# Two transformer layers, twice: all five queues, engine homes and PSUM banks of a written-out order replaced by another table

## The chip, the cores and the metric

One core of a Trainium2 chip runs the whole program. The metric is the device time of one execution in microseconds (us); 442.46 us is the median of three runs of the kernel before (442.39 to 442.56). The profile is one execution taken by the hardware profiler.

## The reference

The input is 2048 tokens of width 512 in bf16. A is sliding-window attention with 32 heads of width 16, B a gelu MLP of width 1792. Both come after a layer norm and are added to the residual:

```python
def _A_ref(x, wqkv, wo):                  # H = 32; Dh = 16; W = 256
    qkv = (x @ wqkv).reshape(B, S, 3, H, Dh).transpose(2, 0, 3, 1, 4)
    q, k, v = qkv[0], qkv[1], qkv[2]
    scores = einsum("bhqd,bhkd->bhqk", q, k) * (Dh ** -0.5)
    mask = (i - j >= 0) & (i - j < W)
    p = softmax(where(mask, scores, -1e9))
    return einsum("bhqk,bhkd->bhqd", p, v).transpose(...).reshape(B, S, D) @ wo
def _B_ref(x, w1, b1, w2, b2):            # 512 -> 1792 -> 512
    return gelu(x @ w1 + b1) @ w2 + b2
x = x + _A_ref(_layernorm(x), wqkv, wo)
x = x + _B_ref(_layernorm(x), w1, b1, w2, b2)
x = x + _A_ref(_layernorm(x), wqkv, wo)   # the same weights again
x = x + _B_ref(_layernorm(x), w1, b1, w2, b2)
```

## The kernel before

Everything stays in SBUF: the residual X (16 tiles of 128 tokens), all weights, and the intermediate buffers. The two repetitions are one stream of 32 tiles, handled as 16 attention blocks (0 to 15) of two tiles; blocks 0 and 8 are the first of a repetition.

For each block the steps are these. Two tiles are normalised on VectorE (statistics L599 and L601, xn L627; the reciprocal root in two small steps, L611 and L617, the second always on GpSimd) and transposed by DMA into xnTA (a few by TensorE). TensorE projects Q, K and V (L653, 256 columns for Q and K, 512 for V). VectorE takes K out of PSUM under a parity mask (KT, L687); Q and V leave PSUM by a copy on VectorE (L588) or on ScalarE (L590). Shifted copies of V go by DMA (Vs). The scores of a block are computed in ten visits (five in blocks 0 and 8), numbered from 0, each a group of small matmuls (L754) into four of the eight PSUM banks. Two exponentials on ScalarE (L761), one for each pair of banks, move a visit to the ring buffer E and free its banks. The window's edges are zeroed by masks (L782) on VectorE or on GpSimd. Two groups of probability matmuls for each block (L804, some 120 matmuls with their sums in a 17th column) write two banks; VectorE transposes them out (OD, L813), takes reciprocals (L817), VectorE or GpSimd normalises (Nb, L821), VectorE transposes back (OT, L827), TensorE projects with Wo (L653, out of OT) and VectorE adds the residual (X, L849).

The MLP runs in ten jobs of two or four tiles: normalisation and transposes into xnTB as above, W1 (L653, ps<-xnTB,W_sb) in 14 groups, gelu into gT (six groups over VectorE's bias add L871 and ScalarE's L874, eight by ScalarE with the bias, L879), W2 (L653, ps<-W_sb,gT, 14 steps for each tile), and the sum X = Xb + ps on VectorE (L894), where Xb, the residual with the bias b2, was prepared on GpSimd (L887). ScalarE changes its function table between exponentials and gelu, 19 loads in all. The last tile is computed in two halves of 256 columns. In the second repetition each finished tile is written out from the SP queue, which issues all DMAs.

What sets the order: the kernel first lists 3098 steps without an order, each with its engine, buffers, the PSUM banks it needs and those it frees. Three tables then decide everything. `_ORDER` is a permutation of the steps; each engine runs its own steps in that sequence. `_ALT` lists the steps that run on their second engine (their home): evacuations VectorE or ScalarE, masks, normalisation and the small L611 VectorE or GpSimd. `_BANKS` gives the first PSUM bank of each group, in the order of `_ORDER`. A step waits, by semaphores, for the last writers of what it reads and the last users of what it overwrites, banks included:

```python
for i in _ALT:
    nodes[i]["eng"], nodes[i]["fn"] = nodes[i]["alts"][1]
...
for i in _ORDER:
    nd = nodes[i]
    for g, k in nd["alloc"]:
        b = next(banks)
        gmap[g] = tuple(range(b, b + k))
    for g in nd["free"]:
        free.update(gmap[g])
```

TensorE has 1629 of the steps; a dense step is one to four matmuls of L653.

Of the kernel before, what the change touches and what calls it, by code (L numbers as in the profile page):

```python
# [19 lines left out]
class _Sched:  # L20
# [147 lines left out]
    15, 34, 5, 0, 6, 14, 35, 7, 33, 28, 38, 29, 47, 8, 18, 23, 9, 36, 3, 26, 31, 10, 57, 37, 11, 22, 1, 40, 4, 24,  # L168
    2, 58, 59, 61, 17, 42, 62, 21, 60, 65, 41, 63, 19, 64, 68, 55, 32, 66, 107, 39, 69, 67, 20, 105, 50, 70, 3097,
    48, 30, 27, 53, 25, 106, 108, 71, 109, 49, 72, 110, 73, 16, 74, 114, 81, 75, 82, 111, 83, 84, 115, 85, 86, 116,  # L170
    112, 87, 88, 89, 113, 195, 153, 117, 127, 128, 151, 196, 129, 130, 154, 118, 152, 131, 119, 197, 155, 120, 156,
    98, 99, 100, 121, 12, 101, 90, 13, 102, 367, 91, 368, 104, 159, 92, 93, 157, 94, 103, 325, 76, 369, 199, 77,
    326, 95, 78, 200, 79, 370, 132, 80, 133, 96, 134, 135, 201, 323, 97, 203, 198, 137, 136, 158, 138, 205, 144,
    139, 202, 140, 145, 204, 141, 146, 160, 147, 122, 520, 217, 148, 123, 206, 124, 219, 143, 125, 208, 126, 46,
    218, 324, 43, 213, 209, 327, 328, 215, 166, 167, 168, 331, 169, 214, 207, 371, 176, 329, 177, 521, 373, 210,
    178, 330, 216, 179, 522, 171, 172, 180, 372, 161, 173, 211, 142, 174, 170, 56, 375, 220, 162, 376, 332, 163,
    164, 523, 175, 524, 221, 374, 377, 150, 212, 165, 149, 380, 378, 222, 188, 382, 189, 44, 190, 181, 45, 525,
    182, 381, 223, 385, 183, 224, 191, 386, 184, 384, 226, 225, 227, 54, 231, 232, 387, 379, 233, 526, 234, 383,
    333, 228, 185, 343, 388, 389, 334, 192, 229, 235, 344, 395, 194, 230, 335, 396, 345, 238, 346, 291, 390, 236,
    397, 239, 237, 347, 240, 336, 241, 348, 337, 349, 338, 242, 350, 244, 339, 243, 391, 399, 351, 401, 340, 341,  # L180
    352, 400, 245, 403, 342, 392, 402, 51, 353, 405, 52, 354, 355, 398, 356, 186, 360, 404, 357, 361, 362, 527,
    363, 393, 408, 364, 253, 409, 260, 261, 407, 254, 262, 410, 359, 413, 255, 246, 247, 415, 411, 256, 412, 257,
    248, 249, 250, 258, 414, 406, 564, 251, 273, 394, 274, 566, 263, 276, 416, 267, 268, 417, 565, 264, 270, 271,
    265, 277, 642, 285, 286, 423, 567, 418, 640, 275, 643, 528, 287, 529, 428, 272, 419, 282, 252, 283, 429, 288,
    259, 289, 641, 420, 308, 290, 309, 421, 424, 266, 310, 311, 279, 278, 644, 269, 422, 645, 284, 307, 280, 312,
    281, 313, 314, 315, 540, 425, 426, 568, 427, 541, 570, 316, 648, 542, 543, 649, 317, 569, 544, 318, 530, 531,
    319, 532, 187, 533, 572, 534, 193, 320, 574, 321, 646, 430, 431, 322, 647, 292, 573, 293, 294, 432, 577, 295,
    435, 579, 366, 576, 296, 545, 297, 436, 358, 571, 298, 433, 578, 546, 582, 434, 547, 437, 584, 548, 575, 550,
    438, 899, 551, 552, 650, 583, 553, 439, 651, 441, 652, 440, 653, 554, 900, 897, 585, 592, 654, 299, 549, 300,
    301, 593, 365, 302, 303, 304, 442, 581, 305, 594, 586, 535, 536, 898, 580, 596, 537, 306, 598, 538, 587, 901,  # L190
    539, 902, 597, 595, 600, 588, 557, 601, 660, 661, 662, 663, 599, 602, 605, 664, 558, 559, 607, 560, 655, 656,
    561, 457, 458, 606, 603, 610, 903, 657, 589, 658, 612, 904, 604, 453, 590, 459, 454, 476, 455, 477, 611, 485,
    486, 563, 609, 479, 591, 480, 482, 562, 613, 659, 470, 471, 483, 556, 905, 464, 465, 467, 478, 468, 484, 608,
    450, 460, 469, 461, 906, 451, 466, 446, 452, 447, 481, 443, 487, 448, 444, 473, 472, 462, 665, 474, 456, 614,
    666, 667, 445, 463, 615, 449, 475, 616, 684, 625, 626, 668, 617, 489, 686, 620, 618, 490, 491, 492, 685, 493,
    619, 621, 494, 669, 688, 687, 627, 690, 628, 622, 629, 495, 488, 623, 689, 496, 632, 692, 497, 694, 498, 624,
    691, 499, 500, 501, 630, 502, 693, 697, 504, 631, 505, 633, 1017, 506, 698, 507, 508, 634, 509, 1018, 510, 503,
    635, 699, 511, 702, 1019, 670, 512, 704, 700, 671, 672, 1020, 695, 673, 1021, 703, 674, 712, 696, 513, 514,
    701, 676, 714, 515, 706, 516, 517, 705, 518, 713, 519, 716, 638, 707, 717, 715, 718, 833, 720, 708, 721, 677,
    917, 1022, 918, 919, 709, 722, 920, 719, 710, 725, 921, 678, 727, 679, 680, 724, 681, 726, 730, 922, 636, 923,  # L200
    1023, 731, 912, 924, 728, 1024, 913, 723, 914, 915, 732, 729, 925, 711, 941, 637, 943, 734, 907, 908, 909, 733,
    910, 916, 926, 555, 735, 942, 639, 1025, 911, 736, 945, 934, 946, 935, 675, 737, 947, 738, 683, 949, 1026, 936,
    739, 948, 951, 937, 740, 938, 741, 742, 682, 950, 743, 944, 954, 744, 745, 955, 746, 747, 750, 952, 748, 940,
    927, 749, 956, 959, 953, 928, 752, 929, 961, 930, 1037, 751, 1038, 753, 931, 1039, 754, 1040, 960, 755, 957,
    969, 970, 756, 758, 757, 963, 971, 973, 962, 1027, 1028, 1041, 974, 1029, 759, 1030, 1031, 958, 977, 978, 964,
    975, 787, 965, 788, 979, 789, 976, 790, 776, 782, 791, 982, 981, 777, 1274, 983, 778, 779, 972, 780, 984, 987,
    980, 783, 784, 988, 785, 966, 986, 765, 786, 766, 767, 985, 768, 989, 771, 769, 772, 773, 774, 991, 1061, 775,
    1063, 990, 1065, 967, 1067, 992, 968, 1062, 1276, 760, 761, 762, 1066, 993, 763, 803, 804, 805, 806, 1068,
    1277, 764, 1069, 798, 1070, 994, 799, 800, 1275, 995, 801, 818, 1071, 819, 820, 821, 1278, 808, 996, 849, 809,
    810, 811, 793, 997, 1279, 998, 999, 770, 794, 1064, 1000, 823, 1001, 795, 807, 796, 1002, 1072, 824, 797, 825,  # L210
    826, 1003, 781, 1004, 1005, 828, 1006, 829, 792, 1032, 1033, 1007, 830, 834, 1034, 822, 1282, 831, 835, 1009,
    1035, 812, 836, 1280, 837, 802, 813, 1010, 814, 1281, 1396, 815, 827, 816, 838, 1073, 839, 1008, 817, 1394,
    840, 1283, 841, 842, 832, 1011, 843, 1012, 844, 845, 1074, 933, 846, 847, 850, 848, 851, 1075, 932, 852, 853,
    1015, 854, 881, 855, 1036, 1076, 856, 1079, 1395, 1397, 857, 1080, 858, 1078, 1077, 859, 860, 882, 861, 1081,
    1089, 862, 863, 1090, 883, 1083, 1082, 884, 885, 864, 886, 1091, 887, 1093, 1042, 1043, 1095, 1092, 1044, 865,
    1045, 1084, 1046, 1094, 1097, 1085, 888, 1098, 889, 890, 891, 866, 1096, 1099, 867, 1086, 1102, 1398, 868,
    1399, 1103, 869, 892, 893, 1100, 894, 870, 1104, 895, 1107, 896, 871, 1109, 872, 1106, 873, 1013, 874, 875,
    1105, 1108, 1014, 876, 1101, 1318, 1402, 877, 878, 1320, 1110, 1111, 1294, 879, 1295, 880, 1296, 1319, 939,
    1297, 1322, 1298, 1016, 1284, 1324, 1285, 1286, 1087, 1287, 1112, 1323, 1288, 1321, 1088, 1326, 1113, 1325,
    1299, 1328, 1300, 1301, 1302, 1289, 1327, 1114, 1331, 1303, 1115, 1290, 1291, 1333, 1292, 1047, 1048, 1293,  # L220
    1330, 1049, 1050, 1332, 1116, 1329, 1336, 1122, 1051, 1123, 1338, 1124, 1125, 1335, 1117, 1126, 1118, 1337,
    1334, 1346, 1119, 1129, 1120, 1348, 1311, 1312, 1121, 1339, 1313, 1314, 1130, 1347, 1127, 1350, 1054, 1055,
    1128, 1315, 1351, 1056, 1131, 1057, 1132, 1058, 1403, 1352, 1354, 1340, 1135, 1356, 1341, 1353, 1136, 1651,
    1355, 1133, 1359, 1342, 1134, 1361, 1304, 1358, 1305, 1306, 1653, 1226, 1307, 1360, 1364, 1308, 1316, 1366,
    1349, 1438, 1060, 1357, 1652, 1362, 1365, 1053, 1164, 1400, 1165, 1166, 1363, 1401, 1167, 1654, 1439, 1368,
    1148, 1149, 1150, 1367, 1151, 1440, 1343, 1059, 1369, 1152, 1344, 1052, 1168, 1655, 1442, 1370, 1210, 1137,
# [739 lines left out]
```

## Time and profile before

| | |
|---|---|
| median of 3 runs | 442.46 us (442.39 to 442.56) |
| span of the profiled execution | 442.4 us |
| TensorE busy (PE) | 416.1 us, 94% |
| ScalarE busy (ACT) | 386.4 us, 87% |
| VectorE busy (DVE) | 341.0 us, 77% |
| GpSimd busy (POOL) | 212.7 us, 48% |
| instruction pages moved by DMA (q8) | 60, 0.98 MB |

The profiled execution's own time is its span, 442.4 us from the first instruction to the last; the runs' times are within 0.2 us of it. PE is TensorE's matmuls, PEld its weight loads, which overlap them; matmuls are pipelined, so a busy PE need not be at its peak. Lines such as L653 are lines of the kernel before; in the kernel after, the tables are eight lines shorter and the same code stands eight lines higher (L653 becomes L645).

### The profile page before, as it was taken

Reading aid. Unit: us, or ns where it says so; the run is one execution under the profiler, and the core shown is the slowest. Engines: PE = TensorE matmul, PEld = TensorE weight load, DVE = VectorE, ACT = ScalarE, POOL = GpSimd, SP = SyncE. Lnnn points to the kernel's source line nnn. Section 1 sums busy time; section 2 is a strip of 40 time slices with the busy share of each in tenths; the row PEclk is TensorE's granted clock in tenths of the full one; section 3 lists DMA queues with packets and bytes.
Section 4 is the critical chain, followed back from the end, with each engine's and each line's share of the span. In section 5 each row is a group of like instructions: output and inputs, shape, how many; then the busy total and the mean of one; then the engine's idle time right before and its main releaser. Section 6 shows DMA issues by size and latency. Waiting matters only on the chain.

```text
span 442.4 us, 16864 instructions
## 1 busy us (share of the span) xinstructions
PE 416.1 (94%) x7523; PEld 233.2 (53%) x7593; DVE 341.0 (77%) x638; ACT 386.4 (87%) x458; POOL 212.7 (48%) x236
## 2 busy tenths in 40 slices
PE   8997999988789997999999999999999999999997
PEld 4555657544444563554455455455555464444675
DVE  7997789788785599967698868877888576746762
ACT  4997999999889999889899989999897988999533
POOL 3566344363442674711575454634728165804411
PEclk9999999999899999999999999999999999999999
DMA  7686422004101012121031021100421014003002
GB/s 234 184 209 185 87 64 45 20 10 69 39 3 25 16 34 56 28 46 24 4 65 31 1 57 26 34 20 10 69 39 20 20 39 105 14 1 81 15 0 73
DMA packets 48116, 23.25 MB, mean 53 GB/s; under 512 B 33196, under 2 KB 48044, under 8 KB 48044
## 3 DMA queue, kind: packets, MB, share of 16 engines
q1 hardware_dynamic: 48044, 22.17, 22.2%
q8 instruction: 60, 0.98, 0.9%
q14 instruction: 12, 0.10, 0.1%
HBM read 8.00 MB, written 2.10 MB: 23 GB/s over the span
## 4 chain that ended last, share of the span: by engine, by line
PE 79%; ACT 11%; DVE 6%; issue 2%; DMA 1%; DVEq 0%
PE ps L653 59%; PE ps L754 9%; PE ps L804 9%; ACT E L761 9%; DVE OD L813 1%; PE ps L539 1%; DVE stat L599 1%; DVE X L849 1%; DMA xnTB<-xn 1%; ACT gT L879 1%; ACT L879 1%; DVE KT L687 1%; DVE E L782 0%; PE ps L639 0%; ACT QT L590 0%
## 5 line engine op out<-in xcount | busy, mean ns | idle before, releaser
L761 ACT ACTIVATE E<-ps 128x1024 bf16<-128x1024 f32 x300 | 284.2, 1033 | 28.7 <-PE ps L754 28.0
L782 POOL TENSOR_TENSOR E<-E,mask 128x512 bf16<-128x512 bf16 (+2 forms) x111 | 120.9, 1106 | 91.3 <-ACT E L761 91.0
L653 PE MATMUL ps<-W_sb,gT 128*128 128x512 bf16 (+1 forms) x434 | 112.2, 373 | 3.2 <-issue 2.2
L653 PE MATMUL ps<-xnTB,W_sb 128*128 128x512 bf16 (+1 forms) x541 | 107.8, 336 | 3.4 <-issue 1.8
L653 PEld LDWEIGHTS ps<-xnTB,W_sb 128*128 128x128 bf16 x560 | 52.0, 98 | 42.9 <-issue 4.1
L653 PE MATMUL ps<-xnTA,Wqkv_sb 128*128 128x256 bf16 x512 | 70.7, 273 | 0.9 <-ACT E L761 0.4
L782 DVE TENSOR_TENSOR E<-E,mask 128x512 bf16<-128x512 bf16 (+2 forms) x125 | 60.1, 500 | 13.3 <-ACT E L761 12.9
L754 PE MATMUL ps<-QT,KT 32*128 32x128 bf16 (+3 forms) x1920 | 60.3, 231 | 9.8 <-ACT E L761 5.6
L653 PEld LDWEIGHTS ps<-W_sb,gT 128*128 128x128 bf16 x462 | 41.2, 98 | 41.1 <-issue 3.6
L754 PEld LDWEIGHTS ps<-QT,KT 32*128 32x128 bf16 x1920 | 28.5, 92 | 59.1 <-ACT E L761 34.9
L653 PEld LDWEIGHTS ps<-xnTA,Wqkv_sb 128*128 128x128 bf16 x512 | 47.4, 98 | 20.2 <-issue 2.9
L813 DVE STREAM_TRANSPOSE OD<-ps 128x1024 f32<-128x1024 f32 x32 | 39.9, 1246 | 21.3 <-PE ps L804 20.7
L887 POOL TENSOR_TENSOR Xb<-X,b2all 128x512 f32<-128x512 bf16 x32 | 37.7, 1180 | 34.3 <-DVE X L894 33.9
L879 ACT ACTIVATE gT<-ps,b1T 128x512 bf16<-128x512 f32 (+1 forms) x80 | 42.6, 609 | 9.5 <-PE ps L653 9.4
L804 PE MATMUL ps<-E,Va 64*17 64x128 bf16 (+3 forms) x1920 | 44.3, 234 | 1.9 <-issue 0.8
L821 POOL TENSOR_TENSOR Nb<-OD,Rc 128x512 bf16<-128x512 f32 x25 | 26.4, 1058 | 38.7 <-DVE Rc L817 29.8
L804 PE MATMUL ps<-E,Vs 64*17 64x128 bf16 (+3 forms) x1920 | 44.9, 234 | 0.0
L599 DVE BATCH_NORM_STATS2 stat<-X 128x6 f32<-128x512 bf16 x64 | 42.9, 679 | 0.5
L804 PEld LDWEIGHTS ps<-E,Va 64*17 64x17 bf16 x1920 | 37.2, 85 | 11.6 <-issue 9.0
L871 DVE TENSOR_SCALAR gT<-ps,b1T 128x512 bf16<-128x512 f32 (+1 forms) x60 | 36.8, 632 | 6.6 <-PE ps L653 6.2
L687 DVE TENSOR_TENSOR KT<-ps,parmask 128x1024 bf16<-128x1024 f32 x32 | 38.7, 1211 | 3.6 <-PE ps L653 3.6
L804 PEld LDWEIGHTS ps<-E,Vs 64*17 64x17 bf16 x1920 | 38.0, 85 | 0.2
(55 smaller groups left out, 348.8 us busy)
## 6 DMA issues: line engine op xcount, KB each, us to landing
Vs<-Va SPq DMA_DIRECT2D x64, 68.0 KB, 2.0
W_sb<-in_B_w_dram SPq DMA_DIRECT2D x4, 512.0 KB, 4.8
out_dram<-X SPq DMA_DIRECT2D x15, 128.0 KB, 1.8
X<-in_A_x_dram SPq DMA_DIRECT2D x3, 512.0 KB
Wqkv_sb<-in_A_wqkv_dram SPq DMA_DIRECT2D x4, 256.0 KB, 4.5
W_sb<-in_B_w_dram SPq DMA_DIRECT2D x2, 384.0 KB, 7.1
W_sb<-in_B_w_dram SPq DMA_DIRECT2D x1, 768.0 KB, 5.0
Wqkv_sb<-in_A_wqkv_dram SPq DMA_DIRECT2D x1, 512.0 KB, 6.7
```

Source lines behind the costliest of these rows:

```text
L599: add("dve", lambda e, B, t=t, k6=k6: e.bn_stats(stat6[:, k6, :], X[:, t, :]), reads=["X%d" % t], writes=["st%d" % k6], key="bs%d" % (k + j))
L653: r = e.matmul(ps[:, B[g][0], cols], lhsT, rhs, start=st, stop=sp)
L687: add("dve", lambda e, B, g=g, i=i: e.tensor_tensor(out=KT[:, kb, 2 * i : 2 * i + 2].rearrange("p c m a q -> p a (c m) q"), in0=ps[:, B[g] ...
L754: x = e.matmul(ps[:, bk[r], o : o + n], KT[rows, kb, c, m].rearrange("p a q -> p (a q)"), QT[rows, c, q : q + n], start=True, stop=True)
L761: add("act", lambda e, B, g_=g_, gi=gi: e.activation(E[:, 2 * gi : 2 * gi + 2, e0 : e0 + 512], ps[:, B[g_][0] : B[g_][0] + 2, :], AF.Exp, ...
L782: fn = lambda e, B: e.tensor_tensor(out=Ew, in0=Ew, in1=Mw, op=ALU.mult)
L804: x = e.matmul(ps[32 * r : 32 * r + VW, B[g][par], c % 2 * 2 * P + lo : c % 2 * 2 * P + hi], V[rows, (2 * b + m // 2) % VR, c * HC + 2 * r ...
L813: add("dve", lambda e, B: e.transpose(OD[:, s].rearrange("p a c q -> p (a c q)"), ps[:, B[g][0] : B[g][0] + 2, :]), reads=["ps:" + g], wri ...
L821: return e.tensor_tensor(out=Nb[:, s, :].rearrange("p (k a d) -> p a k d", a=2, d=Dh), in0=sums[:, :, :, 0:Dh], in1=rc[:, :, :, None].to_b ...
L871: add("dve", lambda e, B, g=g, fc=fc: e.tensor_scalar(out=gT[:, fc, c0 : c0 + M], in0=ps[:, B[g][0], 0:M], scalar1=b1T[:, fc : fc + 1], sc ...
L879: add("act", lambda e, B, g=g, fc=fc: e.activation(gT[:, fc, c0 : c0 + M], ps[:, B[g][0], 0:M], AF.Gelu_apprx_tanh, bias=b1T[:, fc : fc + ...
L887: add("pool", lambda e, B, t=t, xs=xs: e.tensor_tensor(out=Xb[:, xs, :], in0=X[:, t, :], in1=b2all[:], op=ALU.add), reads=["X%d" % t, "b2a ...
```

## The change

The three tables are replaced as a whole; no other line differs. The new order comes from a search that judged an order by the mean over eight sets of durations, with the pages of TensorE's instructions displaced.

```diff
 _ORDER = [
-    15, 34, 5, 0, 6, 14, 35, 7, 33, 28, 38, 29, 47, 8, 18, 23, 9, 36, 3, 26, 31, 10, 57, 37, 11, 22, 1, 40, 4, 24,
...
+    3088, 3089, 2768, 3090, 3091, 3092, 3093, 3094, 3063, 3095, 3096,
 ]
 _ALT = [
-    67, 70, 75, 102, 109, 116, 121, 148, 165, 170, 185, 192, 198, 202, 211, 216, 337, 342, 370, 374, 378, 384, 389,
...
+    67, 70, 75, 102, 109, 113, 121, 148, 165, 170, 185, 192, 198, 202, 207, 211, 216, 337, 370, 374, 393, 402, 406,
...
 _BANKS = [
...
```

In numbers: 46 masks, normalisations and L611 steps move from VectorE to GpSimd and 68 from GpSimd to VectorE (of the masks VectorE had 125 and has 140, GpSimd had 111 and has 96); 8 evacuations move from VectorE to ScalarE and 7 back. ScalarE's 19 table loads stay. Between two neighbouring probability groups TensorE has, but for a few dense steps, the same work as before, in a finer interleaving (1585 rows of like instructions before, 1643 after).

TensorE in block 4, from visit 4 of the scores to the first probability group, before (QT,KT are scores, Wqkv_sb projections):

```order
396 L754 MATMUL ps<-QT,KT 128x128 x8
397 L754 MATMUL ps<-QT,KT 128x64 x16
398 L653 MATMUL ps<-Wqkv_sb,xnTA 128x512 x3
399 L653 MATMUL ps<-xnTA,Wqkv_sb 128x256 x8
400 L754 MATMUL ps<-QT,KT 128x256 x16
401 L653 MATMUL ps<-xnTA,Wqkv_sb 128x256 x8
402 L754 MATMUL ps<-QT,KT 128x192 x8
403 L754 MATMUL ps<-QT,KT 128x128 x4
404 L804 MATMUL ps<-E,Va 17x256 x4
```

and after:

```order
401 L746 MATMUL ps<-QT,KT 128x128 x8
402 L746 MATMUL ps<-QT,KT 128x64 x16
403 L645 MATMUL ps<-Wqkv_sb,xnTA 128x512 x3
404 L645 MATMUL ps<-xnTA,Wqkv_sb 128x256 x2
405 L645 MATMUL ps<-Wqkv_sb,xnTA 128x512
406 L746 MATMUL ps<-QT,KT 128x256 x8
407 L645 MATMUL ps<-xnTA,Wqkv_sb 128x256 x10
408 L746 MATMUL ps<-QT,KT 128x256 x8
409 L746 MATMUL ps<-QT,KT 128x192 x8
410 L746 MATMUL ps<-QT,KT 128x128 x4
411 L796 MATMUL ps<-E,Va 17x256 x4
```

The visits 5 and 6 stood together (row 400) with four dense steps (eight matmuls) behind them; now five dense steps stand between them, and visits 6 and 7 stand together ahead of the probability group.

TensorE right behind that group, before (xnTB is W1's input):

```order
435 L653 MATMUL ps<-xnTB,W_sb 128x512 x6
436 L754 MATMUL ps<-QT,KT 128x192 x8
437 L754 MATMUL ps<-QT,KT 128x128 x4
438 L653 MATMUL ps<-xnTB,W_sb 128x512 x3
439 L754 MATMUL ps<-QT,KT 128x128 x8
440 L754 MATMUL ps<-QT,KT 128x64 x16
441 L653 MATMUL ps<-xnTB,W_sb 128x512 x11
```

and after:

```order
442 L645 MATMUL ps<-xnTB,W_sb 128x512 x4
443 L746 MATMUL ps<-QT,KT 128x192 x8
444 L746 MATMUL ps<-QT,KT 128x128 x4
445 L645 MATMUL ps<-xnTB,W_sb 128x512 x6
446 L746 MATMUL ps<-QT,KT 128x128 x8
447 L746 MATMUL ps<-QT,KT 128x64 x16
448 L645 MATMUL ps<-xnTB,W_sb 128x512 x10
```

Two W1 matmuls moved from ahead of visit 8 to behind it.

VectorE between the second probability group of block 0 and the first of block 1, where the first MLP job's tiles are made ready (E are masks, X the residual sum, stat and statmv the statistics, xn the normalised tiles), before:

```order
50 L827 STREAM_TRANSPOSE OT<-Nb 128x512
51 L782 TENSOR_TENSOR E<-E,mask 128x4x64
52 L627 TENSOR_SCALAR xn<-X,statmv,rstd 128x512
53 L782 TENSOR_TENSOR E<-E,mask 128x4x128
54 L782 TENSOR_TENSOR E<-E,mask 128x4x192
55 L849 TENSOR_TENSOR X<-X,ps 128x512 x2
56 L599 BN_STATS stat<-X 128x6 x2
57 L601 BN_AGGR statmv<-stat 128x2 x2
58 L687 TENSOR_TENSOR KT<-ps,parmask 128x2x8x64
59 L627 TENSOR_SCALAR xn<-X,statmv,rstd 128x512 x2
60 L813 STREAM_TRANSPOSE OD<-ps 128x1024
```

and after:

```order
52 L819 STREAM_TRANSPOSE OT<-Nb 128x512
53 L774 TENSOR_TENSOR E<-E,mask 128x4x128 x2
54 L774 TENSOR_TENSOR E<-E,mask 128x4x64
55 L841 TENSOR_TENSOR X<-X,ps 128x512
56 L774 TENSOR_TENSOR E<-E,mask 128x4x192
57 L841 TENSOR_TENSOR X<-X,ps 128x512
58 L774 TENSOR_TENSOR E<-E,mask 128x4x192
59 L591 BN_STATS stat<-X 128x6 x2
60 L593 BN_AGGR statmv<-stat 128x2 x2
61 L679 TENSOR_TENSOR KT<-ps,parmask 128x2x8x64
62 L619 TENSOR_SCALAR xn<-X,statmv,rstd 128x512 x2
63 L805 STREAM_TRANSPOSE OD<-ps 128x1024
```

Between the transposed output and the statistics stand five masks instead of three (and the mask of row 51 has gone ahead of these rows), and the normalised tile of the next block (row 52 before) has gone behind.

In PSUM, visit 7 of block 1 used banks 0 to 3 and waited for the second exponential of visit 6; it now uses 0, 1, 4 and 5, and the exponential that frees 4 and 5 runs first. At the end, TensorE's last 14 matmuls were those of a full tile (128x512); now they are six of the full tile and then nine of the last half tile (128x256).

364 rows, old and new, of tables (_ALT, _BANKS, _ORDER) are left out of this document.

## The prediction

> **What bounds the kernel now.** I read the page's busy shares first, then its chain of waits, then busy time by stretch, and last the waits inside the stretches that are not full.
>
> The busy shares, and under them the chain that ended last, by engine:
>
> ```profile
> PE 416.1 (94%) x7523; PEld 233.2 (53%) x7593; DVE 341.0 (77%) x638; ACT 386.4 (87%) x458; POOL 212.7 (48%) x236
> ...
> PE 79%; ACT 11%; DVE 6%; issue 2%; DMA 1%; DVEq 0%
> ```
>
> TensorE is the bound, and ScalarE stands close behind it. Busy time by stretch (columns: stretch, length, PE, PEld, DVE, ACT, POOL, granted clock, DMA share, GB/s) says where TensorE is not full:
>
> ```profile
> 80.00:100.00 20.00, 18.01 (x440) 9.25 (x441) 16.94 (x33) 19.34 (x23) 10.83 (x12) 1.00 0.03 6
> 100.00:120.00 20.00, 15.93 (x404) 9.69 (x406) 14.98 (x29) 18.77 (x22) 7.25 (x9) 0.91 0.36 60
> ...
> 160.00:185.00 25.00, 21.90 (x566) 12.38 (x549) 23.80 (x46) 21.93 (x25) 16.97 (x19) 1.00 0.19 39
> 200.00:440.00 240.00, 233.99 (x4012) 126.27 (x4052) 177.77 (x322) 206.27 (x244) 113.59 (x118) 1.00 0.16 33
> ```
>
> From 200 us on TensorE idles 6.0 of 240 us, in short issue gaps: a new order can only lose there. What can be won lies ahead of 200: 4.1 us idle in 100 to 120, 3.1 in 160 to 185, 2.0 in 80 to 100, and a piece at 38 to 44. In the first three ScalarE is nearly full: exponentials pace TensorE through the PSUM banks that they free. The waits between these two:
>
> ```profile
> PEld ps L754 <- ACT E L761: 34.9, 80, 1.5
> ...
> ACT E L761 <- PE ps L754: 28.0, 50, 1.8
> ...
> PE ps L653 <- DMA xnTB<-xn: 0.7, 1, 0.7
> ```
>
> Both wait for each other: a score visit waits for banks that exponentials free, an exponential waits for the next visit. (The third row is needed below.) The worst case of each stands in the same place, by the order in time with the idle time ahead in brackets:
>
> ```profile
> 114.38 0.40 PE L754 MATMUL ps<-QT,KT 32*128 32x256 bf16 x8 [1.25 <-ACT E L761]
> ...
> 121.30 1.94 ACT L761 ACTIVATE E<-ps 128x1024 bf16<-128x1024 f32 x2 [1.78 <-PE ps L754]
> ```
>
> The chain of waits there:
>
> ```profile
> 111.57 4.58 ACT E L761 x5
> 116.16 0.50 ACT QT L590
> 116.66 0.14 issue
> 116.79 2.32 PE ps L804 x125
> 119.11 0.33 issue
> 119.45 1.47 PE ps L653 x5
> 120.92 0.36 PE ps L754 x12
> 121.28 0.02 issue
> 121.30 1.03 ACT E L761
> ```
>
> The probability matmuls (L804) take 2.32 us here. Elsewhere the same work takes 1.37:
>
> ```profile
> 347.50 1.37 PE ps L804 x120
> ```
>
> The reason is the granted clock (last columns but two), in stretches of 3.41 us:
>
> ```profile
> 37.98:41.40 3.42, 2.04 (x29) 1.24 (x31) 2.50 (x3) 3.05 (x4) 1.03 (x1) 1.00 0.40 77
> ...
> 113.08:116.49 3.41, 1.70 (x32) 1.02 (x28) 3.07 (x7) 3.41 (x5) 0.25 (x1) 1.00 0.20 41
> 116.49:119.90 3.41, 2.90 (x138) 2.16 (x132) 0.71 (x1) 3.01 (x4) 1.22 (x2) 0.50 0.20 41
> ```
>
> After a stretch in which TensorE was busy 1.70 us of 3.41 (50%), it ran the next at half clock; after 2.04 us (60%) it did not. [...]
>
> **The change part by part.** The multiset of work stays: 300 exponentials, 19 table loads, the same matmuls, and equally many returns from score or probability matmuls to dense ones. Between the same two probability groups nearly the same dense groups stand, so only waits can move. The sum is made against the profiled execution's 442.4 us, which is the median of the runs (442.46) within 0.1. About 0.2% (0.9 us) is what a measurement of this kernel tells from no change.
>
> *Visits 6 to 8 of block 4 (113 to 121 us).* The change puts the five dense steps ahead of visit 6 instead of four between visits 6 and 7, and four W1 steps instead of six ahead of visit 8. Visit 7 still waits for the first exponential of visit 6, so the pace up to 116.8 stays ScalarE's. Then, at full clock, 1.37 (L804) and four W1 steps, at 0.22 each by this row,
>
> ```profile
> 247.60 7.93 PE ps L653 x36
> ```
>
> end at 116.8+1.4+1.0 = 119.2. Visit 8's new banks are those of both exponentials of visit 7, free at 119.5 (121.30 less the 1.78 that ScalarE waits), so its scores (0.36) end at 119.9 and the exponential starts about 1.3 us earlier. At half clock the chain is 2.32+0.33+4/6 of 1.47+0.36 = 4.0 from 116.8: 120.8, a gain of 0.45. Which one holds hangs on the stretch ahead: the moved steps leave one long wait (1.25 us ahead of visit 6 now, ahead of visit 7 after), so I count 1.7 to 1.95 us of busy time, 50 to 57%, between the two stretches shown. I take the half clock, since 1.70 is the nearer row: -0.45.
>
> *Turn of block 3 to 4 (99 to 107).* Four dense steps that stood ahead of the last probability group of block 3 stand behind visit 1 of block 4, so that group can come up to 0.9 us earlier (4 x 0.22); but visit 2 then needs both exponentials of visit 1 (0.92 each, 4.58 over 5). Between 0 and -0.9 I take -0.2.
>
> *First MLP job (28 to 44).* One chain runs into its first matmul:
>
> ```profile
> 29.05 3.78 ACT E L761 x4
> ...
> 32.86 0.56 DVE E L782
> 33.41 1.20 DVE X L849 x2
> 34.61 1.20 DVE stat L599 x2
> ...
> 36.02 1.11 DVE KT L687
> ...
> 37.23 0.74 DVE xn L627 x2
> ...
> 39.42 4.08 DMA xnTB<-xn
> 43.49 0.09 issue
> 43.58 1.03 PE ps L653 x8
> ```
>
> New here: three masks come from GpSimd to VectorE ahead of the statistics, one normalisation (L627) moves behind them, and the output projection stands without dense steps between its parts, so its second residual sum can start three dense steps (0.65 us) earlier. A mask on VectorE is
>
> ```profile
> L782 DVE TENSOR_TENSOR E<-E,mask 128x512 bf16<-128x512 bf16 x59 | 29.6, 513 | 4.7 <-ACT E L761 4.6
> L627 DVE TENSOR_SCALAR xn<-X,statmv,rstd 128x512 bf16<-128x512 bf16 x64 | 26.6, 431 | 3.2 <-POOL rstd L617 1.6 <-issue 1.2 <-DVE E L782 0.3
> ```
>
> so 3 x 0.51 - 0.43 = +1.1 on VectorE, less the 0.65 from the projection: about +0.4 at the transposes. Against it: the transpose took 4.08 us, and in 41.3 to 42.6 a page of instructions passed beside it,
>
> ```profile
> q8 instruction: 1, 0.02, 4.9%
> ```
>
> where transposes of the other layer norm land in 3.3 at the median of 28:
>
> ```profile
> xnTA<-xn SPq DMA_TRANSPOSE x28, 3.3
> ```
>  Visit 7 of block 1 gets a bank of the first exponential of visit 6 instead of the second, so TensorE reaches the next page up to 0.9 us (one exponential) earlier and the page may miss the transpose: -0.8. Ends +1.1 and -0.9; I take -0.3, a little past the middle of +0.4 and -0.8, since the projection's move is certain and the masks' place in time is not.
>
> *Blocks 6 and 7 (160 to 185).* TensorE's order is the same; one mask goes from VectorE to GpSimd ahead of the first probability group of block 6, and a value projection gets a bank that visit 0 of block 7 does not need. VectorE is busy 23.8 of 25 us there, so a mask (0.51) off its queue counts, at most 0.5: I take -0.25. *Turn of block 2 to 3 (82 to 87):* steps behind the first visit no longer wait for the transposed output, ends 0 and -0.6 (a third of the 2.0 idle in 80 to 100), taken -0.15.
>
> *From 200 us on.* 15 masks net come to VectorE: 7.7 us on an engine with 62 us free in 240, and the evacuations that change between ScalarE and VectorE (8 one way, 7 the other) cancel. What hides them is slack; where it is gone, each costs a wait like the 0.5 ones above. Ends 0 and +1.5 (three of them); I take +0.3.
>
> *The end.* The last matmuls are now a half tile, not a full one:
>
> ```profile
> L894 DVE TENSOR_TENSOR X<-Xb,ps 128x512 bf16<-128x512 f32 x31 | 21.0, 682 | 15.4 <-PE ps L653 15.2
> L894 DVE TENSOR_TENSOR X<-Xb,ps 128x256 bf16<-128x256 f32 x2 | 0.8, 418 | 4.2 <-PE ps L653 4.2
> ```
>
> That is 0.26 less behind the last matmul, but the full tile's sum now stands just ahead of it on VectorE: -0.15. The opening keeps its warm-up and its first loads; the bias load goes behind the projection weights: 0.
>
> Sum: -0.45 -0.2 -0.3 -0.25 -0.15 +0.3 -0.15 = -1.2; rounded towards no change, 441.3 us.
>
> **The rivals.** *The clock stays full through 116 to 120.* For it: the stretch ahead lies between 50 and 60% busy, and the steps ahead bring it forward against the grid. Against it: the ScalarE-paced wait is still 1.2 us. Then the first term is -1.3 instead of -0.45: 440.4 us.
>
> *No change.* The terms at 99 to 107, 82 to 87 and 160 to 185 are small sums of waits that ScalarE paces anyhow; if they come back as waits on the next exponential and the late part costs its +0.3, only -0.45 and -0.15 stand against it: 442.1 us.
>
> *Slower: VectorE in front of the first MLP job.* If the projection gives nothing back, the full +1.1 reaches the transposes, TensorE has nothing left to do ahead of the first W1 step (it waits 0.7 there already), and its busy time of 2.04 us in 37.98 to 41.40 falls towards the 1.70 that halved the clock. Half clock cost 1.3 at 116 us (2.32-1.37 in L804, 1.47-5 x 0.22 in L653). 442.4+1.1+1.3, less 0.7 of the other gains: 444.1 us. It decides from about 0.8 us of delay of the normalised tiles (end of the L627 pair at 37.97 now) on. Against it: the projection's steps do stand closer.
>
> **How the numbers follow.** Forecast 0.33, full clock 0.22: both faster by more than 0.2%, 0.55. No change 0.18. Slower 0.27, into which I put new late waits beyond +1.5 too. The range reaches down past 440.4 by the first job's better end (0.6 more) and the late +0.3 not paid, to 439.4, and up to 444.0, so that some 2 in 10 lie outside.
>
> **What would show it.** Right: no ScalarE wait above 1 us near 120; the first W1 matmuls before 43.6; TensorE's idle time past 200 still near 6 us of 240; behind the last L653 a 128x256 sum. Wrong: a second stretch at clock 0.50, the normalised tiles after 38.7, or waits of TensorE for VectorE past 200.

## The result: slower by 0.4%, and the profile after

The changed kernel takes 443.98 us at the median of 17 runs (442.28 to 445.32), before 442.38 (17 runs, 441.48 to 442.59): ratio 1.004, 95% interval 1.003 to 1.005. Forecast was 441.3.

The profiled execution after took 443.56 us with a span of 441.5 (from the first instruction to the last), so 2.06 us lie outside the span. That matters at once: the span shown of before was 442.4, 0.9 us *longer*. The rows that answer to those of before (in the same views: busy shares, chain by engine, stretches):

```profile
PE 416.4 (94%) x7523; PEld 231.5 (52%) x7593; DVE 342.7 (78%) x659; ACT 387.9 (88%) x459; POOL 191.5 (43%) x214
...
PE 73%; ACT 13%; DVE 6%; DMA 4%; issue 2%; SPq 2%; POOL 0%
```

```profile
80.00:100.00 20.00, 18.07 (x441) 9.52 (x444) 16.28 (x31) 19.47 (x24) 5.12 (x7) 1.00 0.18 23
100.00:120.00 20.00, 15.94 (x429) 9.16 (x421) 18.12 (x36) 18.81 (x22) 7.21 (x9) 1.00 0.32 67
160.00:185.00 25.00, 21.44 (x495) 11.68 (x498) 23.08 (x45) 22.41 (x25) 13.05 (x13) 1.00 0.35 54
200.00:440.00 240.00, 233.85 (x4007) 126.08 (x4046) 175.07 (x330) 207.69 (x245) 102.81 (x108) 1.00 0.16 34
```

New in the chain are DMA (1% before, 4% now) and SyncE's queue (SPq, not there before). Its place is the opening, in the order of time; L694 is a shifted copy of V, L561 and L570 load the second piece of W1 and the first of W2 (512 KB each), L624 issues transposes (in the kernels of the experiments some lines stand one further, L646 for L645):

```profile
25.06 1.45 SPq L694
26.51 0.05 issue
26.56 0.58 SPq L561
27.14 0.05 issue
27.19 0.52 SPq L570
...
27.81 7.06 DMA xnTA<-xn
34.87 0.05 issue
34.92 1.27 PE ps L645 x10
```

The transpose of tile 6 now stands behind two large loads. It is issued at 27.81 us (24.21 in the second profile of before, below) and lands 7.06 us later; TensorE waits 1.7 us for it:

```profile
PE ps L645 <- DMA xnTA<-xn: 1.7, 1, 1.7
```

The stretch of 116 to 120 us is at full clock now (1.00 in the row of 100 to 120, 0.91 there in the first profile of before). The chain there is ScalarE's alone:

```profile
110.97 5.50 ACT E L753 x6
116.47 0.49 ACT QT L582
116.96 2.76 ACT E L753 x3
```

So the repair that was forecast for that place is there, and the kernel still became slower. The first question is then what the 442.4 us of before were.

### The profile page after: what moved, and what is told of

Same layout as the page of the kernel before. It is cut to its first block, busy times and chain, and to the rows that moved or that the text cites. A ratio compares the mean times of both kernels' runs of the same rounds, so it can differ in the third digit from the quotient of the medians.

```text
span 441.5 us, 16867 instructions
## 1 busy us (share of the span) xinstructions
PE 416.4 (94%) x7523; PEld 231.5 (52%) x7593; DVE 342.7 (78%) x659; ACT 387.9 (88%) x459; POOL 191.5 (43%) x214
## 4 chain that ended last, share of the span: by engine, by line
PE 73%; ACT 13%; DVE 6%; DMA 4%; issue 2%; SPq 2%; POOL 0%
PE ps L645 56%; ACT E L753 9%; PE ps L746 9%; PE ps L796 8%; ACT gT L871 2%; DMA xnTA<-xn 2%; DVE E L774 1%; ACT gT L866 1%; DVE OD L805 1%; DVE KT L679 1%; DMA xnTB<-xn 1%; DVE QT L580 1%; DVE OT L819 1%; SPq L694 1%; DMA X<-in_A_x_dram 1%
## 5 line engine op out<-in xcount | busy, mean ns | idle before, releaser
L774 POOL TENSOR_TENSOR E<-E,mask 128x512 bf16<-128x512 bf16 (+2 forms) x96 | 102.0, 1078 | 80.1 <-ACT E L753 80.0
L645 PE MATMUL ps<-xnTB,W_sb 128*128 128x512 bf16 (+1 forms) x542 | 109.7, 335 | 3.2 <-issue 1.6
L645 PE MATMUL ps<-W_sb,gT 128*128 128x512 bf16 (+1 forms) x435 | 110.0, 373 | 2.7 <-issue 2.4
L645 PE MATMUL ps<-xnTA,Wqkv_sb 128*128 128x256 bf16 x512 | 73.9, 273 | 4.0 <-DMA xnTA<-xn 1.7
L645 PEld LDWEIGHTS ps<-xnTB,W_sb 128*128 128x128 bf16 x560 | 51.5, 98 | 41.6 <-issue 2.3
L645 PEld LDWEIGHTS ps<-W_sb,gT 128*128 128x128 bf16 x462 | 41.2, 98 | 41.9 <-issue 3.2
L645 PEld LDWEIGHTS ps<-xnTA,Wqkv_sb 128*128 128x128 bf16 x512 | 46.7, 98 | 26.9 <-issue 3.8
L813 POOL TENSOR_TENSOR Nb<-OD,Rc 128x512 bf16<-128x512 f32 x23 | 24.6, 1068 | 71.9 <-DVE Rc L809 71.3
L871 ACT ACTIVATE gT<-ps,b1T 128x512 bf16<-128x512 f32 (+1 forms) x80 | 43.8, 608 | 10.4 <-PE ps L645 10.2
L609 POOL TENSOR_TENSOR rstd<-rstd,mhalf 128x2 f32<-128x2 f32 x31 | 21.7, 703 | 44.6 <-DVE rstd L603 41.3
```

Of the source, the lines that this page charges most:

```text
L645: r = e.matmul(ps[:, B[g][0], cols], lhsT, rhs, start=st, stop=sp)
L774: fn = lambda e, B: e.tensor_tensor(out=Ew, in0=Ew, in1=Mw, op=ALU.mult)
L813: return e.tensor_tensor(out=Nb[:, s, :].rearrange("p (k a d) -> p a k d", a=2, d=Dh), in0=sums[:, :, :, 0:Dh], in1=rc[:, :, :, None].to_b ...
L871: add("act", lambda e, B, g=g, fc=fc: e.activation(gT[:, fc, c0 : c0 + M], ps[:, B[g][0], 0:M], AF.Gelu_apprx_tanh, bias=b1T[:, fc : fc + ...
```

## The experiments

Theories at the start: **the yardstick** (the profiled execution of before was not a median one), **E** (the loss lies early, in that transpose above all), **L** (it lies past 218 us). A kernel "to step n" takes the first n steps of one table and the rest from the other, with their homes and banks. Times are medians; ratios are against before, run on the same chip beside them (442.19 to 442.36 in all five groups of runs). A kernel's own runs spread by 0.5 to 1.5 us (standard deviation), so a difference of 0.5 us between two medians of 12 is not clear of noise.

### Before again

No edit.

> The kernel before, unchanged, profiled and timed again. Theory 1 (the yardstick was off): the profiled execution of before, span 442.4 us with one stretch of 3.4 us at half clock, was not a median execution; about 2.0 us lie around the span in every run of after, so before's executions at 442.4 us have spans of about 440.4 us and mostly no half-clock stretch. Expect 442.4 us, and a span of about 440.4 where the clock is full throughout. Theory 2 (the yardstick was right): the span of a 442.4 us execution of before is again near 442.4, and the half-clock stretch at 116.5 us is there again; then the 0.9 us that the spans differ by was won, and 1.5 us were lost outside the span.

Measured 442.25 us (12 runs), profiled execution 441.52 with a span of 439.8. Over 29 runs of before beside it, 1.75 us on the mean lie outside the span: an execution of 442.4 us has a span of about 440.6. All 12 are at clock 1.000; of 130 runs of before in all groups 16 have a clock of 0.996 or less, as the first profile had. Its stretches:

```profile
100.00:120.00 20.00, 16.30 (x415) 8.79 (x413) 15.73 (x29) 18.68 (x23) 8.35 (x10) 1.00 0.35 60
160.00:185.00 25.00, 22.75 (x503) 11.54 (x500) 23.85 (x45) 22.99 (x26) 16.79 (x19) 1.00 0.19 38
200.00:440.00 240.00, 236.57 (x4039) 124.64 (x4037) 175.26 (x317) 203.65 (x240) 113.58 (x118) 1.00 0.16 35
```

The yardstick theory holds: the first profile showed an execution of about 444.1 us (an estimate: 442.4 and 1.75), some 1.7 above the median. Its span is 2.6 us longer than this one's, and most of that was lost in two places. Around the half clock (0.50 from 116.49 to 119.90 us) it fell from 1.09 us behind (at the end of block 3's second probability group) to 2.02 and 2.28 (the two groups of block 4). At the first MLP job it fell from 0.31 us behind (block 1's first group) to 1.17 (its second). The last row shows a second trap: past 200 us TensorE idles 3.4 us of 240, not 6.0; the first profile lacked 70 of 7593 matmul records. The profile after lacks 70 too, so its 233.85 us past 200 can't be set beside these 236.57; order_160 (below), which has the changed order there and all its records, has 237.64.

Against this execution the changed kernel's probability groups end as follows (worked out from the traces' signals at the end of each group; in the last column what the stretch added). Both are single executions: 441.52 us is the shortest of the 12 runs of before again, and 443.56 us lies 0.4 below the changed kernel's median.

| up to (time in before) | after minus before | added |
|---|---|---|
| block 1, first group (36 us) | +1.63 | +1.63 |
| block 1, second group (50 us) | +1.15 | -0.48 |
| block 5, first group (148 us) | +0.73 | -0.42 |
| block 7, second group (212 us) | +1.32 | +0.59 |
| last matmul (437 us) | +2.19 | +0.87 |
| end of the execution | +2.04 | -0.15 |

### The halves

```diff
after_to_218:   steps 1-1547 changed, from 1548 on before
after_from_218: steps 1-1547 before, from 1548 on changed
```

> The first 1547 steps (to about 218 us) in the changed order with its homes and banks, all later ones as in before. Theory E (the loss of 1.5 us lies early, such as the transpose of the first query tile that now stands behind two 512 KB weight loads and holds TensorE 1.9 us at 26 to 35 us): 443.6 to 444.2 us. Theory L (the loss lies past 218 us, in more and shorter waits: TensorE's longer ones sum to about 1.5 us there against 0.6): 442.0 to 442.6 us.

Measured 443.17 us (12 runs), ratio 1.0019 (1.0006 to 1.0031).

> The first 1547 steps as in before, all later ones in the changed order with its homes and banks. Theory E: 442.0 to 442.6 us, or 0.3 less if the half tile at the end gives what was forecast. Theory L: 443.6 to 444.2 us.

Measured 444.68 us (5 runs), ratio 1.0052 (1.0039 to 1.0065). Neither theory alone: +0.8 and +2.3 us, both outside what E and L said, and together more than the change's 1.6. The second kernel's profile holds one wait that the changed kernel's has not, for a transpose of the fifth MLP job (the chain):

```profile
230.41 3.97 DMA xnTB<-xn
234.38 0.05 issue
234.43 1.68 PE ps L646 x7
```

TensorE waits 1.42 us for it at 233 us.

### The transpose and the two loads

In tx6_first 45 and 51 are the loads, 330 is the transpose; tx6_late makes the opposite move in before, where the transpose of tile 7 then stands behind the loads as well.

```diff
-    ... 329, 45, 210, 170, 375, 175, 211, 51, 162, 377, 221, 330, 374, ...
+    ... 329, 210, 170, 375, 175, 211, 162, 377, 221, 330, 45, 51, 374, ...
```

> The changed kernel, but on SyncE's queue the transpose of the first query tile stands ahead of the two 512 KB weight loads (first W1 piece 1 and first W2 piece 0) and not behind them. Theory E with the transpose as its cause: TensorE's wait of 1.9 us on it goes, and 1.3 to 1.9 us with it: 442.1 to 442.7 us. Theory E': ScalarE's exponentials pace blocks 0 and 1 and the wait is made up before the first MLP job (in the two traces the same probability group of block 1 ends within 0.1 us of before): 443.7 to 444.1 us, no change against the changed kernel.

Measured 442.93 us (12 runs), ratio 1.0010 (0.9993 to 1.0028): 1.05 less than the changed kernel.

> The kernel before with only this of the change: the two 512 KB loads (first W1 piece 1, first W2 piece 0) stand ahead of the transpose of the first query tile on SyncE's queue. Theory E (this transpose is the main loss): TensorE waits about 1.9 us at 33 to 36 us, and 443.2 to 444.2 us against 442.3. Theory E' (the rest of the changed opening is needed for the loss): 442.3 to 442.7 us.

Measured 444.53 us (12 runs), ratio 1.0042 (1.0027 to 1.0057). The time to landing of the two transposes (tiles 6 and 7), in before again and then in tx6_late, and TensorE's wait in tx6_late:

```profile
DMA to landing us min/median/max: 4.1/4.1/4.1
...
DMA to landing us min/median/max: 6.7/6.7/6.7
...
PE ps L646 <- issue: 1.5, 1, 1.5
```

The wait is named issue there; it ends at 34.2 us, just behind the landing of tile 7's transpose at 34.0 to 34.1. Moved in either direction, the pair changes the time by 1 to 2 us, which speaks for E, though both times lie above what E said. It is not always worth that: both_undone (below) makes the same move in order_160 and isn't faster for it, 442.81 against 442.31 us. In their profiles block 1's first group ends 0.83 us earlier with the move, and its second at the same time within 0.1, so there the wait was made up, as E' said. Behind the two loads the transpose of tile 6 took 7.06 us to land (6.7 in tx6_late), ahead of them 4.1 in before again and 3.9 in tx6_first.

The profile of tx6_first fell on an execution with a half-clock stretch, at another place than before's:

```profile
169.39:172.80 3.41, 1.60 (x36) 0.63 (x34) 3.26 (x9) 3.41 (x5) 0.00 (x0) 1.00 0.45 77
172.80:176.22 3.42, 3.10 (x8) 1.02 (x8) 1.92 (x5) 1.86 (x3) 1.39 (x2) 0.50 0.46 99
```

TensorE's emptiest 3.41 us between 162 and 178 (in steps of 1 us) hold about 2.17 us of matmuls in before again (171.00 to 174.41) and 1.56 in the changed kernel (172.00 to 175.41). 6 of the changed kernel's 17 runs have a clock of 0.996; their median is 444.75, that of the 10 at 1.000 is 443.57.

### Blocks 6 and 7

Five homes first, then the whole order of the stretch:

```diff
six_homes:  -three masks of block 6 and one small step L603 (norm 42, 43) on VectorE, one mask on GpSimd
            +the five as before
order_160:  steps 1-1130 changed, 1131-1270 before, from 1271 on changed
```

> The changed kernel, but five homes of blocks 6 and 7 as before: three masks and one value evacuation back from VectorE to GpSimd, one mask back from GpSimd to VectorE. Theory C (VectorE's queue thins out TensorE's work at 170 to 176 us, where the emptiest 3.4 us hold 1.5 us of matmuls instead of 2.2, so that in some executions the clock halves there): no execution at clock 0.996, the emptiest 3.4 us of 165 to 178 back at 2.0 us or more, and 443.98 us falls by 0.4 to 0.7, to 443.3 to 443.6. Theory C' (the half clock of some executions belongs to another place, or to TensorE's order): about a third of the executions at 0.996 again, 443.8 to 444.1 us.

(The value evacuation named there is in truth the small step L603, L611 in before, of the layer norm of "tiles 42 and 43". Numbers from 32 on are those of the MLP's layer norms: 42 and 43 are tiles 10 and 11, and 46 and 47 below are tiles 14 and 15.) Measured 443.37 us (12 runs), ratio 1.0024 (1.0002 to 1.0046), 2 runs at 0.996. The median is 0.6 lower, but the mean only 0.2 (443.82 against 444.06), and neither C nor C' fits. The longest waits of TensorE between 160 and 180 us stayed:

```profile
PE ps L646 <- DMA xnTB<-xn: 1.2, 1, 1.2
PE ps L797 <- DVE Va L581: 1.0, 1, 1.0
```

> The changed kernel, but steps 1130 to 1270 (about 158 to 178 us) in the order, homes and banks of before. Theory D (there VectorE and GpSimd finish the layer norm of tiles 42 and 43 about 0.9 us too late, since a second mask of 1.6 us stands ahead of its power on GpSimd and another tile's normalisation ahead of its statistics on VectorE, so that the first W1 step of the fourth MLP job waits 1.2 us instead of 0.4, and the stretch is emptied enough for the clock to halve): the wait falls to about 0.5, no executions at 0.996, 443.1 to 443.6 us. Theory D' (these waits are caught up behind, and the half clock belongs to another place): 443.8 to 444.1 us.

Measured 442.31 us (12 runs), ratio 1.0016 (0.9997 to 1.0036), 1 run at 0.996: 1.67 below the changed kernel by the median and 1.2 by the mean (442.84), since 4 of the 12 runs lie at 443.8 or above. That is more than D asked for. The longest waits of the same stretch now:

```profile
PE ps L746 <- DVE Va L580: 0.7, 1, 0.7
PE ps L796 <- DVE E L774: 0.5, 1, 0.5
```

What the stretch changed is seen in the chain of the changed kernel:

```profile
167.35 2.07 DMA Vs<-Va
169.42 0.04 issue
169.46 1.45 PE ps L796 x119
170.91 0.02 issue
170.94 0.46 DVE OD L805
171.40 3.37 DMA xnTB<-xn
174.76 0.09 issue
174.85 1.89 PE ps L645 x8
```

Two transfers end TensorE's waits: a shifted copy of V whose source was ready at 113.7 us but which was issued at 167.35 (140.2 in before again), and the transpose 43. The two normalised tiles come together, at 170.15 and 170.47 us, where before again has them apart, at 168.29 and 169.55: ahead of them stand another tile's normalisation on VectorE and a second mask of 1.6 us on GpSimd. So SyncE's 1.2 us for issuing the first transpose delays the second, which is issued at 171.40 (169.56 in before again). The five homes alone don't bring it back; sequence, homes and banks together do.

### The middle by itself, and the homes by themselves

```diff
middle_only: steps 1-300 before, to 1100 changed, from 1101 on before
homes_late:  changed order and banks; past step 1547 all homes as before
best_one:    after_to_218 with the edits of tx6_first and six_homes
```

> The kernel before, but steps 300 to 1100 (about 37 to 154 us: first MLP job, turns of blocks 2 to 3 and 3 to 4, visits 6 to 8 of block 4) in the changed order with its homes and banks. Theory M (the gains that the prediction named in these places are real): TensorE's waits fall at 38 to 50 us (0.99 at visit 7 of block 1, 0.27 at the first W1 step), at 120 us (0.48 at visit 9 of block 4) and 441.2 to 441.7 us. Theory N (the waits only change place, since ScalarE paces these stretches; 100 to 120 us holds 4.96 us of waits in the changed kernel, 4.55 in an undisturbed execution of before): 442.0 to 442.6 us.

Measured 444.65 us (6 runs), ratio 1.0063 (1.0047 to 1.0078). This tells little: of its loss 1.4 us is a wait for VectorE at 157 us, at the seam of the two orders, and about 1 lies at the other seam, at 38 to 50. Between the seams its groups gain 0.4 us (from +1.28 at 50 us to +0.88 at 148), as in the table above.

> The changed kernel, but past 218 us every mask, normalisation and evacuation on the engine that it had before; the order and the banks stay as changed. Theory H (the 15 masks that came to VectorE cost TensorE the 0.6 to 0.7 us that it waits longer past 218 us): 443.2 to 443.5 us. Theory O (the finer mixing of the order costs it): 443.8 to 444.1 us.

Measured 453.33 us (5 runs), ratio 1.0234 (1.0211 to 1.0257). Neither H nor O: the old homes on the new order cost 9 us more. An order and its homes are one thing, and that a table gives more work to one engine says nothing by itself; H can't be tested so.

> The changed order to 218 us with two edits, the transpose of the first query tile ahead of the two 512 KB loads and the five homes of blocks 6 and 7 as before; past 218 us all as before. If both theories hold and add up: 443.17 (changed to 218 us) less 1.0 and less 0.5, 441.7 us, faster than both kernels, and no execution at clock 0.996. If the two losses are not separate, 442.2 to 442.6 us.

Measured 442.77 us (12 runs), ratio 1.0014 (0.9991 to 1.0038), 4 runs at 0.996 or below, and above both forecasts: with the sequence of 158 to 178 us unmended, the half clock stayed.

### Both undone, and a version that is faster

```diff
both_undone:   order_160 with the edit of tx6_first
both_and_late: steps 1-1130 changed with the edit of tx6_first, from 1131 on before
both_to_238:   both_and_late, but from step 1691 (238 us) on changed
```

> The changed kernel with both undone: the transpose of the first query tile ahead of the two 512 KB loads, and steps 1130 to 1270 (158 to 178 us) as in before. Theory T (these two places are the whole loss, and what the change won between 36 and 150 us remains): 442.31 less 1.0, 441.0 to 441.6 us, faster than before. Theory U (the waits of the second half, 0.9 us, stand against it): 441.8 to 442.4 us, no difference from before.

Measured 442.81 us (12 runs, 440.76 to 444.99), ratio 1.0016 (0.9995 to 1.0037). T is out. No difference from before is what U said, but the median lies 0.4 above its range, and 0.5 above order_160: taking the transpose forward brought nothing on top of that kernel.

> The changed order to step 1130 (158 us) with the transpose of the first query tile ahead of the two 512 KB loads, and everything behind as in before. By the two traces: 0.9 us won between 36 and 150 us, nothing lost behind: 441.3 to 441.8 us, faster than both kernels. If what is won at 36 to 150 us is lost again in the order behind it: 442.1 to 442.5 us.

Measured 441.66 us (12 runs, 440.76 to 442.35), ratio 0.9980 (0.9965 to 0.9994). This beats both kernels, before by 0.6 us. So the first 1130 steps of the changed order, with the transpose put forward, are worth something. Where isn't shown for certain. In its profile (441.66 us) it gains 0.5 us on before again between block 1's first group and block 5's first (from +0.13 to -0.38), where the prediction saw gains, but loses as much by block 5's second (+0.16), at the seam. And none of its 12 runs has a clock of 0.996 or less, against 4 of the 22 of before beside it.

> both_undone, but also steps 1547 to 1690 (218 to 238 us) in the order, homes and banks of before; from 238 us on as changed. There the changed order normalises tile 47 ahead of 46 and issues the last transpose of the fifth MLP job 0.3 to 0.5 us before its first matmul can use it (1.4 us in before); in the profile of after_from_218 that matmul waits 1.42 us for it, and 5 of both_undone's 12 executions lie 1 to 2 us above its others. Theory X (this thin margin is missed in part of the executions, and that is most of what the second half loses): no execution above 443.2 us, median 441.7 to 442.1 us. Theory Y (the second half loses by its small waits at 307 to 407 us, 1.0 us in all): 442.4 to 442.9 us.

Measured 442.16 us (12 runs, 441.68 to 443.57), ratio 0.9992 (0.9977 to 1.0006), no longer faster than before. The run differs from both_undone by more than the text above says: all of steps 1131 to 1690 (158 to 238 us) are in the order of before, 1271 to 1546 too. Much of the spread of both_undone is gone (5 of 12 runs above 443.2 there, 1 here), and 0.65 us of the median with it, which alone is not clear of noise. X comes nearest, though its bounds are just missed; its direct sight is the 1.42 us wait in after_from_218, while the profile of both_undone (442.40 us) has no such wait at 225 to 240 us. The rest (0.5 us against both_and_late) stays with the changed order behind 238 us, where small waits stand.

### The pages of TensorE's instructions

The edits put more instructions ahead of TensorE's work, so that other instructions of it should stand where a page ends. Two matmuls replaced by 32 are 30 matmuls and 30 weight loads more (one load for each matmul: 7593 and 7593 on the page of both_and_late), eight replaced by 136 are 256 instructions more.

```diff
pages_60, pages_60_before: 2 of the 18 warm-up matmuls
-    one matmul of 512 columns
+    sixteen of 32 columns
pages_256: 8 of the 18
-    one matmul of 512 columns
+    seventeen of 30 columns
```

> [...] Past 205 us the changed kernel has gaps of 0.1 to 0.22 us inside probability groups at fixed places (307.5, 328.5, 361.5, 374.1, 406.6 us), each shortly ahead of the fetch of a page; together with their neighbours 1.5 us against 0.5 in before. Theory P (page boundaries inside the groups cause them): the gaps stand elsewhere or go, and the sum of waits past 205 us changes by 0.3 us or more, either way. Theory Q (they belong to the order of the work): the same gaps at the same places, 443.7 to 444.2 us.

Measured 457.38 us (4 runs), ratio 1.0347 (1.0332 to 1.0361). The forecast named the wrong waits: the gaps at 307 to 407 us stood where they had been. From the first to the last weight load, the probability groups that begin at 306, 360 and 405 us take 1.49, 1.30 and 1.41 us in the changed kernel, 1.46, 1.30 and 1.41 here and 1.17 each in before again, so the gaps belong to the order, as Q said. But new and larger waits came, in the middle of a group of small matmuls whose inputs are all there. The chain of pages_60:

```profile
50.29 1.35 PE ps L797 x109
51.64 1.80 issue
53.44 0.34 PE ps L797 x11
```

```profile
243.02 0.19 PE ps L747 x4
243.22 1.99 issue
245.21 0.32 PE ps L747 x8
```

The DMA view of 242 to 244.5 us holds one page of instructions, at 242.3 to 242.4 us and so just ahead of the stop, and copies of V from 244.3 us on:

```profile
q8 instruction: 1, 0.02, 3.6%
```

> The kernel before, with the edit of pages_60: two warm-up matmuls of 512 columns are each 16 of 32, so that all pages of TensorE's instructions begin 60 instructions earlier in the work. Theory V (any table that was tuned at one position of its pages loses by a displaced one, in waits of 1 to 2 us for the next page in the middle of a group, with half clock behind some): 450 to 460 us. Theory W (only the changed order is sensitive): 442 to 443.5 us.

Measured 456.93 us (6 runs), ratio 1.0326 (1.0292 to 1.0360): V. Both tables lose alike, and in part at the same count of TensorE's weight loads and matmuls, though the work there differs: both profiles have a stop behind 7020 of them (2.1 and 1.9 us), behind 8539 or 8540 (2.2 and 1.6) and behind 11072 or 11076 (0.9 and 1.2; all from start to start).

> The changed kernel, with eight warm-up matmuls of 512 columns each as 17 of 30 columns: 256 instructions more, one whole 16 KB page, so that every page boundary falls on the same instructions of the work as in the changed kernel. Theory P (what cost pages_60 its 13 us is where the page boundaries fall): 443.5 to 444.8 us. Theory R (it was the longer opening or the many short matmuls there): 455 us or more.

Measured 445.00 us (10 runs), ratio 1.0049 (1.0029 to 1.0069), with 61 pages fetched instead of 60. That is 0.2 above P's range and 10 below R's: P. The same kind of edit with four times as many instructions costs 12 us less (445.00 against 457.38). A page holds about 253 instructions, by an estimate from the page of both_and_late (15186 matmuls and weight loads on 60 pages, if these hold TensorE's alone). The place of the pages as the cause fits both times, but no view shows where a page ends in the work. The number of instructions ahead of the work is part of what a table was timed with.

## Why the prediction was wrong

**The failed step** is "the sum is made against the profiled execution's 442.4 us, which is the median of the runs (442.46) within 0.1". It set a span beside a time. The profiled execution took about 444.1 us, and the two largest terms (-0.45 and -0.3) were read at the places where that execution had lost about 1 us each. The changed kernel's profiled execution, 443.56 us, is 0.6 faster than that and 1.2 slower than the median of before. From 444.1 the sum of -1.2 would have given 442.9; the 1.1 us from there to the measured 443.98 are terms that the sum had at nothing or with the wrong sign, the opening and blocks 6 and 7.

**Visits 6 to 8 of block 4** (-0.45, or -1.3 at full clock). Against an execution at full clock there is nothing to win: up to block 3's second group the changed kernel is +0.97 behind before again, up to block 4's second +1.07. The sign called "right" (no wait of ScalarE above 1 us near 120) came true and was worth nothing. The rival that kept the clock full (440.4 us) was right about the clock, and forgot that before has it full too.

**The opening** ("0"). This is the other failed step: it looked at the first loads on SyncE's queue and not at the transposes among the later ones. Against before again it cost 1.6 us by the first group of block 1, of which the first MLP job gave some back; tx6_first and tx6_late show 1.05 and 2.3 in the time, and both_undone against order_160 shows nothing.

**First MLP job** (-0.3): -0.48, right in size. The rival that put a loss here, VectorE's masks ahead of it, gave 444.1 us and so the right time by luck: the normalised tiles come at 38.1 us, 0.4 later than in before again, while the transpose in the opening had already cost 1.6.

**Blocks 6 and 7** (-0.25): +0.59, and in part of the executions the half clock as well. The prediction said that TensorE's order is the same and one mask leaves VectorE. In the tables a few dense steps of TensorE change place too, and for the one mask of block 6 that leaves VectorE three come to it, two of them ahead of the first probability group. It had not looked at SyncE's queue or at VectorE's sequence there; order_160, which takes the stretch back, takes the loss back.

**Turn of block 2 to 3** (-0.15): the second group of block 2 gains 0.25 on that of block 1. **Turn of 3 to 4** (-0.2): 0.07 lost.

**Past 200 us** (+0.3, ends 0 and 1.5): +0.87 from 212 us on, inside its bounds, though 11 of the 15 masks and not all come to VectorE past step 1547 (218 us). In the runs a thin margin may count too (both_to_238), which one profile can't show. The sign for "right", TensorE idle near 6 us past 200, came true (6.15) and says nothing, since both profiles lack records. **The end** (-0.15): from the last matmul to the end of the execution 4.74 us in before again and 4.58 after, -0.16. Right.

The range held the time by 0.02 us (443.98 against 444.0), which is luck. The chances of 0.55 for faster rested on an execution with a half-clock stretch, as only 1 run in 8 of before has by its clock.

**The rule for the clock.** The prediction read one stretch of 3.41 us after another: 1.70 us of matmuls (50%) halves the next one's clock, 2.04 us (60%) does not. The runs show that the busy time alone doesn't decide. In tx6_late 2.06 us was followed by half clock and 1.77 us, two stretches later, was not; what else decides was not shown:

```profile
105.92:109.34 3.42, 2.06 (x37) 0.76 (x30) 1.84 (x3) 2.38 (x4) 1.32 (x2) 1.00 0.69 82
109.34:112.75 3.41, 3.41 (x20) 1.17 (x19) 2.17 (x4) 2.31 (x3) 3.41 (x4) 0.50 0.55 80
112.75:116.16 3.41, 3.23 (x48) 1.60 (x45) 2.89 (x7) 3.41 (x5) 1.13 (x3) 1.00 0.05 12
116.16:119.58 3.42, 1.77 (x28) 1.04 (x29) 3.00 (x6) 3.40 (x5) 0.08 (x1) 1.00 0.26 52
119.58:123.00 3.42, 3.41 (x148) 2.15 (x149) 1.94 (x3) 2.83 (x4) 1.59 (x2) 1.00 0.15 29
```

Where the stretches lie is an estimate from the traces' records of the clock: within a trace its changes lie whole multiples of 3.413 us apart (32 and then 1 from 7.26 us on in the first profile of before, 128 in the changed kernel's). In the first profile of before the clock falls at 116.49 us; in before again, whose clock rises at 4.80 us, stretches counted on from there begin at 114.0 and 117.4. So where the emptiest moment falls in these stretches differs between these profiles: in tx6_first one with 1.60 us ran ahead of half clock, while in the changed kernel's profile (clock up at 5.37 us, down at 442.27) the one from 172.62 to 176.04 us holds 1.73 us and the clock stayed full.

## What to carry to other kernels

Compare a span only with spans, and look first whether the profiled execution is a typical one: add what lies outside the span, look at the clock, and count the matmul records. When an order is replaced, walk the DMA queue's sequence before the engines': here, in the traces, a transpose behind two 512 KB loads and a stretch in which two transfers came late cost more than all gains on the engines. And measure an order that is tuned to a few tenths of a percent again when instructions are added to TensorE's stream: sixty cost 3% here.

## What the runs showed of the hardware

Sixty more instructions ahead of TensorE's work cost 13.4 us (changed) and 14.7 us (before), 3%; 256 more, with 61 pages fetched instead of 60, cost 1.0. In pages_60 TensorE stood still for 1.8 and 2.0 us in the middle of groups, the second time from 0.8 us behind the fetch of one page; the profile names such waits issue.

Stretches of 3.41 us with 1.60, 1.70 and 2.06 us of matmuls were followed by half clock, those of 1.73, 1.77 and 2.04 us were not. The clock rose at 7.26, 4.80 and 5.37 us in three profiles (the two of before, the changed kernel's), and within one its changes lie whole multiples of 3.413 us apart. And equal kernels differ by more than the three first runs let see: before lies between 441.2 and 445.0 us in 130 runs, not within 0.17.
